# Block-sparse attention with a gated feed-forward: edge rows scored by four 64 by 64 tiles in two halves with a running maximum, and the next batch's keys loaded three units sooner

## Chip, cores and metric

One core of one Trainium2 chip runs the whole program in one launch. The metric is device time in microseconds (us).

## What is computed

Attention with a block mask over 4 batches, 8 heads, 768 positions of width 64 in 24 blocks of 32, and then a gated feed-forward over all 3072 tokens (width 512, inner width 2048):

```python
mask = np.abs(blk_i - blk_j) <= window                      # window = 1
mask = mask | (blk_i == 0) | (blk_j == 0) | (blk_i == n_blocks - 1) | (blk_j == n_blocks - 1)
for qb in range(n_blocks):
    for kb in sampled_blocks[qb]:                           # 3 random blocks of each
        mask[qb * block:(qb + 1) * block, kb * block:(kb + 1) * block] = True
scores = np.where(mask, scale * q @ k.T, -1e9)
attn = softmax(scores)
x = attn @ v                                                # heads side by side: 512 wide
h = x @ w_in
g = h * erf(maximum(h, 0) + log1p(exp(-abs(h))))            # softplus inside erf
out = g @ w_out
```

The 22 middle blocks of queries see eight blocks of keys each. The first and the last block see all 768 keys; these 64 queries of each head are the edge rows.

## The kernel before

**Units.** Each batch is cut into 15 units, in this order: eleven middle units (`"m"`, two middle blocks of queries, all eight heads) and four edge units (`"f"`, one pair of heads each). Below, m0 to m10 are the middle units of a batch and f0 to f3 its edge units; the m0 of the next batch follows f3. A unit goes through these steps: `scores` (L613) has TensorE write f32 scores into the tile `s`, of which there is only one buffer (`ps_s`, `bufs=1`); `soft_max` (L557) has VectorE reduce them to the negated row maxima `less`; `soft_exp` (L566) has ScalarE write `pf = exp(s + less)` and the f16 high part `p`; `soft_low` (L602), one group of the feed-forward later, has VectorE write the f16 low part of `p` and SyncE issue the transposing DMA to `pT`. Three units later `values` (L643) multiplies `pT` with the gathered values into `po`, and `norm` and `turn` make the transposed input `xT` of the feed-forward of it. The two first edge units are answered by `values` together, and so are the two last ones.

**Scores of an edge unit.** Queries and keys lie with two heads on the 128 partitions (64 rows each). For an edge unit a tile `qm`, zero off its diagonal blocks, holds the edge queries of both heads of a pair side by side; `order_q` (L167) fills it once a batch. One matmul of full height and width gives 128 rows (two heads by 64 queries) for 512 keys, a second one those for the last 256 keys (`scores`, the `else` branch). In f32 each of these stands as two instructions in the trace. Middle units use 64 by 32 tiles of the array (eight at a time).

**Groups.** The feed-forward runs in 96 groups (4 batches, 3 chunks, 8 groups). Group m does `ff_first` (24 matmuls into `h`, three buffers), `ff_logs` (five activations of ScalarE: tiles `x` and `y`), `ff_power` (VectorE, `y<-y,x`), `ff_exp` (ScalarE, `y<-y`); two groups later `ff_gate` (VectorE, `y<-y,h`, then two instructions that write `g`), which frees the buffer of `h`; three groups later `ff_second` (12 matmuls into `o`). Of some groups `ff_store` has ScalarE write `wi` or `wo` from `o` and send them out.

**Order of the work.** From the fourth group on (`held[0]`, L983) every engine keeps the order in which the loop from L978 on is written; for the queues of SyncE and GpSimd that holds from the beginning, and before that point a scheduler may move instructions of the other engines. A table (`until`, `spread`, L968 to L975) says which groups carry a unit. A group with a unit runs through

```python
values; ff_first; ff_logs; gathers; scores; ff_second; ff_gate; soft_low(the unit before)
norm; soft_max; turn; ff_power; soft_exp; ff_exp; next_queries; behind
```

so on ScalarE the two activations of `soft_exp` stand between the five of `ff_logs` and the one of `ff_exp`, and on VectorE `soft_low` stands ahead of `soft_max` and `ff_power`.

**The next batch.** `behind` (L853) prepares batch c while batch c - 1 runs. Values: `load_v` (768 KB, ScalarE's DMA queue), `max_v`, `scale_v`, and four `split_v`, at units m10, f0, f2 and f3, each with two activations of ScalarE and two instructions of VectorE into the tile `vn` (one buffer) and a store to a table in memory. Keys: `load_k` (L123) loads four tiles `kr` (384 KB each, one a unit, ScalarE's DMA queue) and `order_k` (L134) has GpSimd copy each into `kx` one unit later. `k_from` (L851) sets the first load at m9; `v_from` sets the first load of values at m6. `kr` has its room in the ring of `pf` (two buffers). When all four are copied, `gathers` may copy random blocks of keys from `kx` into `kbuf`. The `kx` of the second batch lies in the buffer `room`, which holds constants and scratch of the start.

## Time and profile before

| what | us |
|---|---|
| median of 3 runs | 773.09 |
| lowest and highest of them | 768.38, 774.7 |
| the profiled execution: its own time | 770.67 |
| its span, first to last instruction | 768.8 |
| TensorE (PE) busy | 689.5 |
| ScalarE (ACT) busy | 591.9 |
| VectorE (DVE) busy | 575.3 |
| GpSimd (POOL) busy | 202.1 |

The span is that of the profiled execution; 1.87 us of its own time lie outside it. Busy time is the time in which an instruction of the engine ran; TensorE's ends are modelled, since matmuls overlap. PEld is TensorE's loading of weights, and a name with a q (ACTq, SPq) is the sequencer that issues DMAs. Every row carries the line L48, a helper's, so instructions are told apart by the tiles they write and read (`out<-in`). What the names mean: `s_m` and `s_f` are scores of middle and edge units, `po` the attention output, `h` and `o` the two products of the feed-forward.

### The profile page before, as it was taken

What the parts mean: (1) busy time and instruction counts of PE and PEld (TensorE: products, weight loads), DVE (VectorE), ACT (ScalarE), POOL (GpSimd) and SP (SyncE); (2) the same over time, 40 slices, a digit from 0 to 9 for tenths busy, and PEclk for the clock granted to TensorE, in tenths of its full rate; (3) what the DMA queues carried; (4) which work ended last, traced back from release to release, by engine and by line L of the source; (5) the groups of instructions that cost most, each with busy time, mean ns of one, the idle gap of its engine ahead of it and who ended that gap; (6) DMA issues with size and microseconds to landing.
All of it is one profiled execution on the core that took longest, in us unless ns stands there. A gap on an engine that the chain in (4) does not pass through costs nothing.

```text
span 768.8 us, 24885 instructions
## 1 busy us (share of the span) xinstructions
PE 689.5 (90%) x10400; PEld 451.1 (59%) x10400; DVE 575.3 (75%) x1122; ACT 591.9 (77%) x1023; POOL 202.1 (26%) x413
## 2 busy tenths in 40 slices
PE   1347896999899999999899999999999999999997
PEld 0224464656466665666566666666666666667663
DVE  6985999887768878777777878777777786664453
ACT  3546899878868878788878887878878887786774
POOL 3027532214343322031533322033433120000000
PEclk9757997999999999999999999999999999999999
DMA  9999835996799898745988899727979786130000
GB/s 319 411 279 289 248 101 130 195 235 166 145 204 195 209 190 192 189 116 121 227 176 192 169 195 193 210 62 191 214 151 190 137 152 153 42 71 8 8 29 27
DMA packets 188048, 129.36 MB, mean 168 GB/s; under 512 B 137760, under 2 KB 160928, under 8 KB 186912
## 3 DMA queue, kind: packets, MB, share of 16 engines
q1 hardware_dynamic: 173584, 84.50, 52.7%
q10 hardware_dynamic: 8464, 25.43, 10.2%
q0 software_dynamic: 5888, 17.84, 9.1%
q8 instruction: 81, 1.33, 0.7%
q14 instruction: 31, 0.25, 0.1%
HBM read 82.81 MB, written 12.95 MB: 125 GB/s over the span
## 4 chain that ended last, share of the span: by engine, by line
PE 64%; DVE 10%; ACT 8%; DMA 8%; issue 5%; SPq 2%; ACTq 1%; POOL 0%; POOLq 0%; DVEq 0%
PE h L48 26%; PE o L48 25%; PE s_m L48 6%; PE po_None L48 3%; DMA vtab<-vn 3%; DMA vbuf<-vtab 3%; ACT x L48 2%; SPq L48 2%; PE s_f L48 2%; DVE y L48 2%; DVE vn L48 1%; ACT pf_m L48 1%; DMA qt<-in_qT_dram 1%; ACT wi L48 1%; DVE room L48 1%
## 5 line engine op out<-in xcount | busy, mean ns | idle before, releaser
L48 PE MATMUL h<-xT,wi 128*128 128x256 f16 x2304 | 270.7, 274 | 10.5 <-DVE y L48 9.4
L48 PE MATMUL o<-wo,g 128*128 128x512 f16 x1152 | 265.8, 381 | 0.5 <-DVE g L48 0.2
L48 PEld LDWEIGHTS <-wi 128*128 128x128 f16 x2304 | 223.2, 98 | 50.6 <-issue 7.3
L48 ACT ACTIVATE x<-x 128x512 f32<-128x512 f32 x288 | 181.6, 632 | 8.8
L48 PEld LDWEIGHTS <-g 128*128 128x128 f16 x1152 | 109.9, 98 | 129.0 <-issue 10.0
L48 POOL DMA_INDIRECT vbuf<-vtab,idx x88 | 93.8, 1066 | 186.9 <-PE po_None L48 128.1
L48 DVE SCALAR_TENSOR_TENSOR y<-y,x 128x512 f32<-128x512 f32 x96 | 66.9, 697 | 82.0 <-ACT x L48 78.8
L48 POOL COPY kbuf<-kx 128x128 f32 (+1 forms) x280 | 90.3, 367 | 97.1 <-PE s_m L48 82.5
L48 ACT ACTIVATE x<-h,isg 128x512 f32<-128x512 f32 x96 | 65.4, 682 | 50.7 <-PE h L48 32.8
L48 ACT ACTIVATE y<-y 128x512 f32<-128x512 f32 x96 | 59.8, 623 | 36.9 <-DVE y L48 36.9
L48 ACT ACTIVATE pf_m<-s_m,less_m 128x256 f32<-128x256 f32 x176 | 68.9, 473 | 20.9 <-DVE less_m L48 20.9
L48 DVE SCALAR_TENSOR_TENSOR g<-y,sums,g 128x512 f16<-128x512 f32 x96 | 73.0, 761 | 3.4
L48 DVE SCALAR_TENSOR_TENSOR y<-y,h 128x512 f32<-128x512 f32 x96 | 65.1, 678 | 0.1
L48 ACT ACTIVATE y<-x 128x512 f32<-128x512 f32 x96 | 60.5, 631 | 3.0
L48 DVE TENSOR_REDUCE less_m<-s_m 128x4 f32<-128x1024 f32 x44 | 53.5, 1216 | 12.2 <-PE s_m L48 12.2
L48 PE MATMUL s_m<-kbuf,qt 64*32 64x160 f32 x1408 | 51.1, 321 | 4.7 <-issue 3.8
L48 PE MATMUL s_m<-kx,qt 64*32 64x96 f32 x1408 | 31.9, 260 | 23.8 <-ACT kx L48 13.8
L48 PEld LDWEIGHTS <-pT_m 128*32 128x32 f16 x3168 | 35.3, 98 | 28.3 <-issue 25.2
L48 DVE TENSOR_SCALAR g<-y,sums 128x512 f16<-128x512 f32 x96 | 49.2, 512 | 3.4
L48 PE MATMUL po_None<-vbuf,pT_m 128*32 128x65 f16 (+2 forms) x3168 | 41.9, 205 | 7.5 <-issue 7.5
L48 DVE SCALAR_TENSOR_TENSOR p_m<-pf_m,p_m 128x1024 f16<-128x1024 f32 x38 | 46.3, 1218 | 0.6 <-ACT p_m L48 0.6
L48 DVE TENSOR_TENSOR x<-xf,x 128x256 f16<-128x256 f32 x44 | 18.7, 424 | 33.5 <-ACT x L48 33.4
(110 smaller groups left out, 609.9 us busy)
## 6 DMA issues: line engine op xcount, KB each, us to landing
vbuf<-vtab SPq DMA_DIRECT2D x80, 195.0 KB
vraw<-in_v_dram ACTq DMA_DIRECT2D x9, 768.0 KB
vtab<-vn SPq DMA_DIRECT2D x16, 390.0 KB
vbuf<-vtab SPq DMA_DIRECT2D x12, 520.0 KB
wo<-in_w_out_dram ACTq DMA_DIRECT2D x6, 1024.0 KB
qt<-in_qT_dram SPq DMA_DIRECT2D x20, 256.0 KB
kr<-in_kT_dram ACTq DMA_DIRECT2D x12, 384.0 KB
vbuf<-vtab SPq DMA_DIRECT2D x32, 130.0 KB
```

Of the source, the lines that this page charges most:

```text
L48: done = call(*args, **kwargs)
```

## The change

Edge units change in what they hold. A pair of units now covers four heads (two pairs of heads): the even one (f0, f2) scores the first 512 keys, the odd one (f1, f3) the last 256. Each has four matmuls of 64 rows and 64 columns, one for each quarter of the array, read from the queries as loaded; `qm` and `order_q` are gone. The maximum runs: the odd unit takes the smaller `less` of the two, and `drop`, the exponential of the difference (two tiny activations), scales the even unit's `pf`. The f16 high parts of both units are now written in the odd unit's `soft_exp`, both low parts and both transposes come in its `soft_low`, and the even unit has only its exponentials.

```diff
-        dve.tensor_reduce(less, s.rearrange("p (g w) -> p g w", w=width), AX.X, ALU.max, negate=True)
-        dve.tensor_scalar(less, less, D**-0.5, None, ALU.mult)
-        softs[unit] += (less,)
+        dve.tensor_reduce(less, s.rearrange("p (g w) -> p g w", g=groups)[:, :, :width], AX.X, ALU.max, negate=True)
+        if unit[0] == "m" or unit[2] % 2 == 0:
+            dve.tensor_scalar(less, less, D**-0.5, None, ALU.mult)
+            softs[unit] += (less,)
+            return
+        first = softs[unit[0], unit[1], unit[2] - 1][-1]
+        dve.scalar_tensor_tensor(less, less, D**-0.5, first, ALU.mult, ALU.min)
+        dve.tensor_tensor(first, less, first, ALU.subtract)
+        softs[unit] += (less, first)
...
+        if rest:
+            drop = st.tile([P, 2], F32, tag="drop", name=f"drop_{tag}", bufs=1)
+            act.activation(drop, rest[0], AF.Exp)
+            act.activation(drop, drop, AF.Copy, scale=P_SCALE)
...
+            for who, src, scale in ((before, softs[before][0], drop), (unit, pf.rearrange("p (g w) -> p g w", w=width), None)):
...
+                if scale is None:
+                    act.activation(p3[:, :, 0], src, AF.Copy, scale=P_SCALE)
+                else:
+                    for g in range(2):
+                        act.activation(p3[:, g, 0], src[:, g], AF.Copy, scale=scale[:, g : g + 1])
...
+        if unit[0] == "f":
+            if unit[2] % 2 == 0:
+                return
+            for n, (who, p2, p3, src, scale) in enumerate(softs.pop(unit)):
+                if scale is None:
+                    dve.scalar_tensor_tensor(p3[:, :, 1], src, P_SCALE, p3[:, :, 0], ALU.mult, ALU.subtract)
+                else:
+                    for g in range(2):
+                        dve.scalar_tensor_tensor(p3[:, g, 1], src[:, g], scale[:, g : g + 1], p3[:, g, 0], ALU.mult, ALU.subtract)
+                pT = at.tile([P, 16, P], F16, tag="pT", name="pT_" + "_".join(str(x) for x in who), bufs=3)[:, : p2.shape[1] // P]
+                sp.dma_start_transpose(out=pT, in_=p2)
...
-            q_ = qm[:, n].rearrange("p n a c -> p (n a c)")
-            for c, e in ((0, 512), (512, S)):
-                keys = kx[:, c // BLOCK : e // BLOCK, n, :]
-                pe.matmul(s[:, c:e], q_, keys, start=True, stop=True)
-            softs[unit] = (s[:, :S], 1, S)
+            qt = queries(b, NU).rearrange("p r j c -> p r (j c)")
+            first, last = ((0, 16), (16, NB))[n % 2]
+            width = (last - first) * BLOCK
+            for a in range(2):
+                pr, o = n // 2 * 2 + a, slice(a * D, (a + 1) * D)
+                for r in range(2):
+                    d = slice(r * D, (r + 1) * D)
+                    keys = kx[d, first:last, pr, :]
+                    pe.matmul(s[o, r * 512 : r * 512 + width], qt[d, pr], keys, start=True, stop=True)
+            softs[unit] = (s, 2, width)
```

The keys of the next batch start at m6, as its values do, and their tiles `kr` move from the ring of `pf` to the one buffer of `vn`. In `behind` a copy of keys now stands ahead of the steps for values.

```diff
-            kr = at.tile([P, 1024], F32, tag="pf", name=f"kr_{b}_{pr}", bufs=2)[:, :S]
+            kr = at.tile([P, S], F32, tag="vn", name=f"kr_{b}_{pr}", bufs=1)
...
-    k_from = {c: 9 if c == 1 else c * per - 6 for c in range(1, B)}
+    k_from = v_from
```

How the order stands now, at three places. ScalarE in the group that carries f3 of the first batch (`wo` and `out_dram` are the store before it, `x_1_3` and `y_1_3` its group, `vn` the split of values), before and then now:

```order
186 L48 ACTIVATE wo<-o_1_1874,iso_1_2904 128x512
187 L48 DMA out_dram<-wo 128x512
188 L48 ACTIVATE x_1_3_2933<-h_1_3_2908,isg_1390 128x512
...
191 L48 ACTIVATE x_1_3_2933<-x_1_3_2933 128x512
192 L48 ACTIVATE pf_f_3_3007<-s_f_3_2982,less_f_3_3003 128x768
193 L48 ACTIVATE p_f_3_3009<-pf_f_3_3007 128x768
194 L48 ACTIVATE y_1_3_2937<-y_1_3_2937 128x512
195 L48 ACTIVATE vn_0_1_3012<-vraw_0_2687,s_v_2314 128x6x64 x2
```

Now the same group reads:

```order
195 L48 ACTIVATE x_1_3_2981<-h_1_3_2956,isg_1388 128x512
...
198 L48 ACTIVATE x_1_3_2981<-x_1_3_2981 128x512
199 L48 ACTIVATE drop_f_3_3016<-less_f_2_2879 128x2
200 L48 ACTIVATE drop_f_3_3016<-drop_f_3_3016 128x2
201 L48 ACTIVATE pf_f_3_3019<-s_f_3_2988,less_f_3_3011 128x256 x2
202 L48 ACTIVATE p_f_2_3022<-pf_f_2_2887,drop_f_3_3016 128x512 x2
203 L48 ACTIVATE p_f_3_3025<-pf_f_3_3019 128x2x256
204 L48 ACTIVATE y_1_3_2985<-y_1_3_2985 128x512
205 L48 ACTIVATE vn_0_1_3028<-vraw_0_2737,s_v_2321 128x6x64 x2
```

Between the last of the logarithms and `y` stood two activations and stand seven now. VectorE in the next group, from the two instructions that write `g` to the maxima of m0 of the next batch (`po_11_0`, `xf_11` are the norm of f0 and f1), now:

```order
318 L48 SCALAR_TENSOR_TENSOR g_1_2_3210<-y_1_2_2927,sums,g_1_2_3210 128x512
319 L48 SCALAR_TENSOR_TENSOR p_f_2_3022<-pf_f_2_2887,drop_f_3_3016,p_f_2_3022 128x512 x2
320 L48 SCALAR_TENSOR_TENSOR p_f_3_3025<-pf_f_3_3019,p_f_3_3025 128x2x256
321 L48 TENSOR_SCALAR rinv_11_0_3220<-po_11_0_3035 128x2
...
325 L48 TENSOR_REDUCE less_m_0_3226<-s_m_0_3164 128x4
326 L48 TENSOR_SCALAR less_m_0_3226<-less_m_0_3226 128x4
327 L48 SCALAR_TENSOR_TENSOR y_1_4_3161<-y_1_4_3161,x_1_4_3157 128x512
```

Before, one instruction of 768 columns (`p_f_3`) stood where these three of 512 stand. ScalarE at the start of the program, where the scheduler still moves instructions (`raw` and `wo` are loads of weights, `kr_0` the first load of the second batch's keys), now:

```order
23 L48 DMA raw_284<-in_w_out_dram 128x1024
24 L48 ACTIVATE sq_i_501,sums<-wi 128x1024
25 L48 DMA wo<-in_w_out_dram 128x2x1024
26 L48 DMA kr_0_1471<-in_kT_dram 128x768
27 L48 ACTIVATE sq_i_684,sums<-wi 128x1024
28 L48 ACTIVATE pf_m_2_628<-s_m_2_592,less_m_2_625 128x256 x4
```

Row 26 is new there; before, that load stood in the group of m9.

## Rows read from the trace of the kernel before

**Rows 1.** Page, part 1: busy time, share of the span and instructions.
```profile
PE 689.5 (90%) x10400; PEld 451.1 (59%) x10400; DVE 575.3 (75%) x1122; ACT 591.9 (77%) x1023; POOL 202.1 (26%) x413
```
**Rows 2.** Busy time by stretch: us, then each engine; clock, DMA share, GB/s last.
```profile
300.00:345.00 45.00, 43.46 (x483) 28.92 (x481) 33.87 (x69) 36.00 (x60) 8.46 (x21) 1.00 0.66 163
625.00:680.00 55.00, 54.99 (x612) 36.26 (x610) 39.13 (x77) 44.23 (x73) 1.42 (x2) 1.00 0.51 103
55.00:60.00 5.00, 0.69 (x12) 0.28 (x3) 1.74 (x2) 0.00 (x0) 4.08 (x10) 0.50 1.06 263
```
**Rows 3.** Waits of TensorE: who waited for whom, us in total, times, longest.
```profile
PE h L48 <- DVE y L48: 9.4, 4, 4.5
PE s_m L48 <- ACT pf_m L48: 5.4, 3, 2.7
```
**Rows 4.** TensorE in order of time: start, duration, xcount; second batch, m7 and f0.
```profile
261.75 0.56 PE L48 MATMUL s_m<-kx,qt 64*32 64x96 f32 x32
...
309.28 1.46 PE L48 MATMUL s_f<-kx,qm 128*128 128x512 f32 x4
310.57 2.75 PE L48 MATMUL o<-wo,g 128*128 128x512 f16 x12
```
**Rows 5.** Loading of weights around the same two units; idle before in brackets.
```profile
261.75 0.35 PEld L48 LDWEIGHTS s_m<-kx,qt 64*32 64x32 f32 x32 [0.21 <-issue]
...
263.11 0.33 PEld L48 LDWEIGHTS <-g 128*128 128x128 f16 x3 [0.25 <-issue]
...
309.18 0.30 PEld L48 LDWEIGHTS s_f<-kx,qm 128*128 128x128 f32 x2
```
**Rows 6.** Groups by shape: busy us, mean ns of one, idle before.
```profile
L48 ACT ACTIVATE pf_f<-s_f,less_f 128x768 f32<-128x768 f32 x16 | 14.2, 890 | 5.2 <-DVE less_f L48 5.2
L48 ACT ACTIVATE p_f<-pf_f 128x768 f16<-128x768 f32 x16 | 13.5, 843 | 0.5
L48 ACT ACTIVATE x<-x 128x512 f32<-128x512 f32 x288 | 181.6, 632 | 8.8
L48 ACT ACTIVATE x<-xf 128x256 f16<-128x256 f32 x44 | 17.7, 402 | 4.2 <-DVE xf L48 4.1
L48 DVE TENSOR_REDUCE less_m<-s_m 128x4 f32<-128x1024 f32 x44 | 53.5, 1216 | 12.2 <-PE s_m L48 12.2
L48 DVE TENSOR_REDUCE less_f<-s_f 128x1 f32<-128x768 f32 x16 | 15.2, 950 | 0.3 <-PE s_f L48 0.3
L48 DVE SCALAR_TENSOR_TENSOR p_f<-pf_f,p_f 128x768 f16<-128x768 f32 x16 | 15.3, 955 | 0.0
L48 DVE COPY qm<-qt 64x256 f32<-64x256 f32 x8 | 2.3, 285 | 0.1
```
**Rows 7.** In order of time, first border: f3 of batch 0 to the next m1.
```profile
187.03 1.46 PE L48 MATMUL s_f<-kx,qm 128*128 128x512 f32 x4
...
190.28 0.69 ACT L48 ACTIVATE x<-h,isg 128x512 f32<-128x512 f32 x1 [0.43 <-ACT wo L48]
...
195.71 1.10 ACT L48 ACTIVATE vn<-vraw,s_v 128x384 f16<-128x384 f32 x2
...
196.41 1.18 DVE L48 SCALAR_TENSOR_TENSOR vn<-vraw,s_v,vn 128x384 f16<-128x384 f32 x2 [2.07 <-ACT vn L48]
...
199.44 0.95 DVE L48 SCALAR_TENSOR_TENSOR p_f<-pf_f,p_f 128x768 f16<-128x768 f32 x1
...
202.79 1.57 ACT L48 ACTIVATE pf_m<-s_m,less_m 128x256 f32<-128x256 f32 x4 [2.75 <-DVE less_m L48]
...
204.41 0.56 PE L48 MATMUL s_m<-kx,qt 64*32 64x96 f32 x32 [2.71 <-ACT pf_m L48]
```
**Rows 8.** In order of time, second border: the group of m0 and the next m1.
```profile
360.58 0.63 ACT L48 ACTIVATE y<-y 128x512 f32<-128x512 f32 x1 [0.92 <-DVE y L48]
...
368.24 0.56 PE L48 MATMUL s_m<-kx,qt 64*32 64x96 f32 x31 [0.79 <-issue]
```
**Rows 9.** Chain that ended last, at the start of the program: start, us, what.
```profile
52.76 8.99 DMA vbuf<-vtab
```

More of the change, by code (lines that the diff above doesn't have):

```diff
@@ L145, in sparse_attention_moe @@
     qts = {}
-    qm = cp.tile([P, HP, 2, 2, BLOCK], F32, tag="qm", name="qm")
-    dve.memset(qm, 0.0)
     def load_q(b, t):
@@ L165, in queries @@
         return qts[b, t][:, :, half * 2 * BLOCK : (half + 1) * 2 * BLOCK].rearrange("p r (j c) -> p r j c", c=BLOCK)
-    def order_q(b):
-        qt = queries(b, NU)
-        for a in range(2):
-            dve.tensor_copy(qm[a * D : (a + 1) * D, :, :, a, :], qt[a * D : (a + 1) * D])
     QW = 4 * VW
@@ L561, in soft_max @@
         less = st.tile([P, 4], F32, tag="less", name=f"less_{tag}")[:, :groups]
-        dve.tensor_reduce(less, s.rearrange("p (g w) -> p g w", w=width), AX.X, ALU.max, negate=True)
-        dve.tensor_scalar(less, less, D**-0.5, None, ALU.mult)
-        softs[unit] += (less,)
+        dve.tensor_reduce(less, s.rearrange("p (g w) -> p g w", g=groups)[:, :, :width], AX.X, ALU.max, negate=True)
[7 more added lines that the diff above has]
+        softs[unit] += (less, first)
     def soft_exp(unit, early=False):
-        s, groups, width, less = softs[unit]
+        s, groups, width, less, *rest = softs[unit]
         tag = "_".join(str(x) for x in unit)
         n = groups * width
+        if rest:
+            drop = st.tile([P, 2], F32, tag="drop", name=f"drop_{tag}", bufs=1)
+            act.activation(drop, rest[0], AF.Exp)
+            act.activation(drop, drop, AF.Copy, scale=P_SCALE)
         pf = at.tile([P, 1024], F32, tag="pf", name=f"pf_{tag}", bufs=2)[:, :n]
@@ L573, in soft_exp @@
             c = slice(g * width, (g + 1) * width)
-            act.activation(pf[:, c], s[:, c], AF.Exp, bias=less[:, g : g + 1], scale=D**-0.5)
+            act.activation(pf[:, c], s.rearrange("p (g w) -> p g w", g=groups)[:, g, :width], AF.Exp, bias=less[:, g : g + 1], scale=D**-0.5)
         if early:
             softs[unit] = (s, groups, width, pf)
+            return
+        if unit[0] == "f":
+            if not rest:
+                softs[unit] = (pf.rearrange("p (g w) -> p g w", w=width), less)
+                return
+            before = unit[:2] + (unit[2] - 1,)
+            parts = []
+            for who, src, scale in ((before, softs[before][0], drop), (unit, pf.rearrange("p (g w) -> p g w", w=width), None)):
+                w = src.shape[2]
+                p2 = at.tile([P, 2048], F16, tag="p2", name="p2_" + "_".join(str(x) for x in who), bufs=2)[:, : 4 * w]
+                p3 = p2.rearrange("p (g a w) -> p g a w", a=2, w=w)
+                if scale is None:
[3 more added lines that the diff above has]
+                        act.activation(p3[:, g, 0], src[:, g], AF.Copy, scale=scale[:, g : g + 1])
+                parts.append((who, p2, p3, src, scale))
+            del softs[before]
+            softs[unit] = parts
             return
@@ L602, in soft_low @@
     def soft_low(unit):
+        if unit[0] == "f":
+            if unit[2] % 2 == 0:
+                return
+            for n, (who, p2, p3, src, scale) in enumerate(softs.pop(unit)):
[6 more added lines that the diff above has]
+                sp.dma_start_transpose(out=pT, in_=p2)
+                pts[unit[0], unit[1], unit[2] // 2, n] = pT
+            return
         p2, p3, pf3, n = softs.pop(unit)
@@ L665, in values @@
                             else:
-                                pT = pts["f", b, pr][:, x * KT + k]
+                                pT = pts["f", b, p2_, k // 4][:, r * (8 - k // 4 * 4) + x * (4 - k // 4 * 2) + k % 4]
                                 vg = vgs[b, -1 - k // 2][:, k % 2, w]
-                                col = j * 64 + r * BLOCK
+                                col = a * 64 + j * BLOCK
                             todo.append((2 * a + j, pT[:, col : col + BLOCK], vg, at_gr + off))
@@ L836, in next_queries @@
         b, n = divmod(m, per)
-        if n == NU - 1:
-            order_q(b)
         if n < NU - 1 and n % 2 == 0 and (b or n >= 6):
@@ L850, in sparse_attention_moe @@
     v_from = {c: 6 if c == 1 else c * per - 9 for c in range(1, B)}
-    k_from = {c: 9 if c == 1 else c * per - 6 for c in range(1, B)}
+    k_from = v_from
     def behind(m):
         for c in range(1, B):
+            n = m - k_from[c]
+            if 1 <= n < 5:
+                order_k(c, n - 1)
             e = m - v_from[c]
@@ L868, in behind @@
                 have_v.add(c)
-            n = m - k_from[c]
-            if 1 <= n < 5:
-                order_k(c, n - 1)
             if 0 <= n < 4:
```

## Prediction

> **What bounds the kernel now.** I read the busy times first, then the stretches with edge units, then TensorE's waits, and last, in order of time, the borders between batches. TensorE is busy 689.5 of 768.8 us, ScalarE 591.9 [rows 1]. In the edge units of the second batch TensorE works 43.46 of 45 us and ScalarE 36.00; in those of the last batch TensorE works 54.99 of 55 [rows 2]. So TensorE sets the pace, ScalarE is the next engine, and TensorE's waits for others are few: 9.4 us of `h` for a gate of VectorE, 5.4 us of `s_m` for the exponentials that free the one score tile [rows 3]. The question is where these few waits stand: all that TensorE gains ahead of such a wait is lost in it, if what it waits for comes no earlier.
>
> They stand at the borders between batches. At the first one the scores of m1 begin at 204.41, 2.71 us after TensorE was free, when the exponentials of m0 end (202.79 + 1.57 = 204.36) [rows 7]. Those wait for the maxima of VectorE (2.75 us), and VectorE had been held up by `vn`, for which it waited 2.07 us on ScalarE. ScalarE was late already: the scores of f3 begin at 187.03, when TensorE has issued the `h` of that group, but ScalarE takes that `h` at 190.28. At the second border m1 begins at 368.24 after 0.79 us without work [rows 8]; the third repeats it. The last batch has no border behind it.
>
> **TensorE's scores.** An edge unit takes from 309.28 to 310.57, 1.29 us for 768 columns [rows 4], 1.68 ns a column, so 0.86 us for 512 and 0.43 for 256. Do four tiles of 64 by 64 run side by side? The trace shows the neighbouring case: 32 instructions of 96 columns (16 matmuls, eight tiles) take 0.56 us with the tail of the last one [rows 4], while 16 x 96 columns one after the other would take 2.58. So they do, and a pair of units costs 0.86 + 0.43 = 1.29 us where it cost 2.58. With eight pairs that is 10.3 us less. But the weights of the small tiles wait before and after: loading stands idle for 0.21 us ahead of `s_m` and 0.25 behind it, while `s_f` is loaded 0.30 us without a gap [rows 5]. Part of that lies under running matmuls. I take 0.2 us a unit, between nothing and the full 0.46: a pair then saves 1.29 - 0.4 = 0.89, eight pairs 7.1 us (10.3 to 2.9 by the bounds).
>
> The Trainium skill, TensorEngine Tiling (Array Packing), Tiling Modes, says that changing the tiling mode, not just the tile, drains TensorE. The two gaps agree with it, and it speaks against this change: edge units ran in the mode of the feed-forward and would now leave it and come back. Without a drain the sum below would be 0.8 us lower.
>
> **ScalarE.** Before, an edge unit has an exponential of 768 columns (0.89 us) and a copy (0.84) [rows 6], together 1.73. The even unit now has two exponentials of 512, like `x<-x` at 0.63: 1.26, 0.47 less. The odd unit has two of 256 (four take 1.57 [rows 7], so 0.79), three copies of 512 columns (between the 0.40 of 256 and the 0.84 of 768: 0.62 each, 1.86), and two activations of two columns, which no row shows: each costs something between nothing and the 0.40 of 256 columns, and since a fixed part stays I take 0.2. That makes 3.05, 1.3 us more (0.9 to 1.7). A pair costs ScalarE 0.85 us more, in all 6.8 us, off the path as long as ScalarE is not the one waited for.
>
> **VectorE.** Reductions cost 1.216 us for 1024 columns and 0.950 for 768, so 0.68 for 512; the low part costs the same a column (0.955 for 768) [rows 6]. The even unit reduces 0.27 us longer and has no low part (0.955 less). The odd one reduces 0.27 us shorter, adds one tiny instruction, and has three low parts of 512, 2.05 us, 1.1 more. The eight copies into `qm` go (0.285 each); they are followed by `vn`, for which VectorE waits on ScalarE [rows 7], so I count them at nothing, and at most at 2.3 us if that wait is gone.
>
> **What reaches the end, border by border.**
>
> First border. ScalarE's start at 190.28 hangs on a store and the `g` of VectorE, not on TensorE, which is 3 us ahead; what f0 to f2 saved on TensorE does not move it. From there to `vn` at 195.71 ScalarE runs without a pause, so the odd unit moves `vn` by +1.3, and with it VectorE's `vn`, gate and `g`. Then come the low parts at 199.44, 1.1 us longer. The maxima and exponentials of m0, and so m1 at 204.41, come 2.4 us later (0.9 if the small pieces cost nothing and part is caught up, 3.2 at worst).
>
> Second and third border. By the table of units two groups without a unit lie between f1 and f2 and one between f3 and the border, so I take ScalarE to have caught up with TensorE at f2, whose `h` then comes earlier by what f0 and f1 save (0.4 and 0.8, less a little: 1.1). In f3 the odd unit takes 1.3 back, and the longer low parts (1.1) stand ahead of the `y<-y,x` for which ScalarE's `y` waits 0.92 [rows 8]. That is about +0.8 there, of which roughly 0.5 goes into later waits of ScalarE for TensorE's scores: +0.3 each, +0.6 for both (-1.0 to +2.4 each).
>
> Last batch. No border, no split of values, no wait [rows 2]: two pairs at 0.89 give -1.8 (-2.6 to -0.7).
>
> Start. Between loads of weights ScalarE now issues the first keys of the second batch: 128 x 768 x 4 bytes, 393 KB. At that time DMA is full (share 1.06, 263 GB/s [rows 2]) and the chain runs over DMA, the 8.99 us of values for m0 from 52.76 on [rows 9]. 393 KB at 263 GB/s are 1.5 us; some of it goes ahead of that stretch, so I take 1.0 (0 to 3, since the issue itself waits for a store from `vn`, with ScalarE's work queued behind it, and the order of the start is dealt anew).
>
> The Trainium skill, Trainium Kernel Development and Optimization, Key Constraints, says that DMAs from SP, ACT and POOL queues all run on the same 16 engines and interleave. The full share agrees; by it the whole 1.5 us would come out of the start, and the sum would be 0.5 us higher.
>
> Later keys. The loads leave the edge units for m6 to m9, and `kr` has one buffer: a load cannot be issued until GpSimd has copied the tile before, and behind the issue on ScalarE stands the next group. The worst case is the second load, since the first follows 768 KB of values: 1.18 MB at 263 GB/s take 4.5 us, and from f3 to m1, two units, there are 17.4 us [rows 7], so one unit is some 8.7. It fits. I count nothing; if it misses by 2 us three times, ScalarE loses 6 us while TensorE is ahead.
>
> **Sum.** 770.67 + 2.4 + 0.6 - 1.8 + 1.0 = 772.9 us. The profiled execution lies 2.4 us below the median of the runs shown, which spread over 6.3 us, so the forecast is no change: 772.9. A measurement of this kernel can tell about 1% (7.7 us) from no change.
>
> **The rivals.**
>
> *TensorE keeps its saving everywhere.* Then 7.1 us come off: 763.5, and 760.4 without any drain. For it speaks that ScalarE is busy only 36 of 45 us [rows 2] and that `h` waits 9.4 us in the whole run [rows 3]. Against it: the scores of m1 wait for ScalarE at every border already [rows 7, 8], and nothing in the change brings those exponentials forward. It would need ScalarE to catch up 2 us between f3 and m0. Chance 0.17.
>
> *The odd units' tail becomes the bound.* Seven activations and three low parts in one group hold the gate and the next maxima at every border as at the first, and the odd f1 also delays what follows it: 3 x 2.4 + 3 x 1.3 + 1.5 at the start - 1.8 = +10.8, 781.5. It decides from the point at which ScalarE has no pause left between f3 and m0; at the second border 0.92 us of it show [rows 8], at the first none. Against it: after f1 comes a group without a unit in the later batches. Chance 0.18.
>
> *The tiles do not overlap.* If four small matmuls run one behind the other, each as long as a full one, a pair takes 5.16 us and not 2.58: 8 x 2.58 = +20.6, 791.3. Against it stands the row of `s_m` [rows 4]; for it only that no row shows tiles 64 columns wide. Chance 0.03.
>
> **How the numbers follow.** The forecast has the rest, 0.62, and is the only case within 1%. Faster by over 1% is the first rival, 0.17, slower the other two, 0.21. The range goes from 763.5, the saving kept with its drain, to 781.5, the tail at every border; left out are a saving without drain, tiles that do not overlap and a start that costs more than 3 us. The forecast's own range is 768 to 778.
>
> **What the profile after would show.** Right: from the start of `s_f` to the next `o` about 1.06 us in even and 0.63 in odd units; three copies of about 0.62 us in the odd one; at the first border a wait of `s_m` for `pf_m` well over 2.71 us, at the others longer than 0.79; the edge units of the last batch without a wait. Wrong: if m1 begins earlier after f0 than now, counted from m10, then ScalarE had the room and the first rival holds; if `s_f` takes over 1.29 us, the third; if `h` waits for gates several times 9.4 us, the second; if ScalarE stands before m8 or m9 with a load of keys as its releaser, the later keys were not free.

## The result and the profile after

The change takes 777.59 us, median of 13 runs, against 773.09 for the kernel before, also of 13: a ratio of 1.007, 95% interval 1.0046 to 1.0093. One of its 13 executions, at 785.46 us, ran in a slower state; without it the means are 0.6% apart. The change is some 5 us slower than the kernel before: inside the range and inside the 1% that the prediction named, but the interval leaves no doubt of the sign, and the forecast was 772.9 us, no change. Measured again, beside other kernels (e11 below), the ratio was 1.0055 (1.0030 to 1.0080). The profiled execution took 776.47 us, 5.8 more than that of before; its span is 774.7 us, of before 768.8.

The page of after, part 1, answers to [rows 1]:

```profile
PE 680.4 (88%) x10464; PEld 441.2 (57%) x10464; DVE 576.8 (74%) x1129; ACT 597.7 (77%) x1063; POOL 199.6 (26%) x413
```

TensorE has 9.1 us less to do, ScalarE 5.8 us more. All that TensorE was spared is gone, and 5.9 us on top. To find where, the starts of the scores in the two traces are set side by side, unit by unit:

| scores of | before, us | after, us | behind by | gained (-) or lost since the row above |
|---|---|---|---|---|
| f0, first batch | 153.46 | 160.61 | 7.15 | +7.15 |
| f3, first batch | 187.03 | 195.08 | 8.05 | +0.90 |
| m1, second batch | 204.41 | 213.98 | 9.57 | +1.52 |
| f0, second batch | 309.28 | 320.66 | 11.38 | +1.81 |
| f3, second batch | 347.85 | 356.92 | 9.07 | -2.31 |
| m1, third batch | 368.24 | 378.06 | 9.82 | +0.75 |
| f0, third batch | 475.03 | 484.21 | 9.18 | -0.64 |
| f3, third batch | 513.83 | 521.91 | 8.08 | -1.10 |
| m1, fourth batch | 534.25 | 543.05 | 8.80 | +0.72 |
| f0, fourth batch | 639.54 | 647.00 | 7.46 | -1.34 |
| f3, fourth batch | 676.51 | 683.06 | 6.55 | -0.91 |
| end of the span | 768.8 | 774.7 | 5.9 | -0.65 |

The whole loss is there before the first edge unit has begun. What the edge units and borders do afterwards adds up to a small gain. A single row is good to 1 or 2 us only: those from m1 to the next f0 hold no edge unit, and they moved by +1.81, -0.64 and -1.34. In a second trace of the change (e11) the first f0 is 7.64 us behind and the end 5.5. In order of time, TensorE of before and then of after, where the feed-forward begins:

```profile
101.87 3.44 PE L48 MATMUL h<-xT,wi 128*128 128x256 f16 x30 [0.55 <-DVE xT L48]
```

```profile
110.75 5.07 PE L48 MATMUL h<-xT,wi 128*128 128x256 f16 x45
```

The first `h` comes 8.9 us later. The stretch ahead of it, 60 to 90 us (us, then busy time of PE, PEld, DVE, ACT, POOL; clock, DMA share, GB/s), of before and then of after:

```profile
60.00:90.00 30.00, 24.21 (x510) 14.11 (x509) 23.97 (x52) 23.69 (x48) 20.65 (x40) 0.89 1.04 296
```

```profile
60.00:90.00 30.00, 21.70 (x420) 11.68 (x420) 18.49 (x37) 19.05 (x38) 15.99 (x30) 0.76 0.87 245
```

Every engine works 2.4 to 5.5 us less in the same 30 us. What they wait for stands in order of time. Before, 58 to 67 us (`po_None` is the first product with values, `rest` a product of weights, the POOL row the seventh gather of values):

```profile
59.41 2.73 ACTq L48 DMA_DIRECT2D wo<-in_w_out_dram  x2
59.48 0.21 PE L48 MATMUL po_None<-vbuf,pT_m 128*32 128x65 f16 x1 [4.31 <-issue]
...
62.25 1.47 ACT L48 ACTIVATE wi<-wi,sums 128x512 f16<-128x512 f32 x2 [8.91 <-DMA vbuf<-vtab]
63.02 0.58 PE L48 MATMUL rest<-wi,room 128*128 128x512 f16 x1 [2.33 <-ACT wi L48]
...
64.25 1.49 PE L48 MATMUL po_None<-vbuf,pT_m 128*32 128x65 f16 x71
...
66.06 0.97 POOL L48 DMA_INDIRECT vbuf<-vtab,idx  x1 [3.34 <-PE po_None L48]
```

After, 48 to 75 us:

```profile
48.95 0.35 ACTq L48 DMA_DIRECT2D kr<-in_kT_dram  x1
...
58.66 6.47 ACTq L48 DMA_DIRECT2D wo<-in_w_out_dram  x2
...
65.23 1.48 ACT L48 ACTIVATE wi<-wi,sums 128x512 f16<-128x512 f32 x2 [11.59 <-DMA vbuf<-vtab]
66.00 0.58 PE L48 MATMUL rest<-wi,room 128*128 128x512 f16 x1 [10.98 <-ACT wi L48]
...
67.23 0.23 PE L48 MATMUL po_None<-vbuf,pT_m 128*32 128x65 f16 x1
...
67.40 2.50 PE L48 MATMUL rest<-wi,room 128*128 128x512 f32 x3
...
70.55 1.34 PE L48 MATMUL rest<-wi,room 128*128 128x512 f32 x2
...
71.82 0.88 PE L48 MATMUL po_None<-vbuf,pT_m 128*32 128x65 f16 x71
...
73.04 1.81 POOL L48 DMA_INDIRECT vbuf<-vtab,idx  x1 [10.37 <-PE rest L48]
```

Three things are new. The load of keys (`kr`) is out at 48.95, ahead of five of the six loads `wo`. ScalarE's `wi` starts when two of those are issued (62.25 after 59.41 + 2.73 before, 65.23 after 58.66 + 6.47 now), so it seems to stand behind its own sequencer, whatever releaser the row names. And between the first matmul with values and the other 71, which free the buffer for the next gather, TensorE now has five matmuls of weights (67.40 and 70.55) where it had two; that gather starts at 73.04 instead of 66.06. At this point the load and the order are two suspects with one trace; GpSimd's early copy of these keys will be a third.

The edge units themselves. TensorE in the last batch, f2 and f3, answers to [rows 4]:

```profile
676.72 1.09 PE L48 MATMUL s_f<-kx,qt 64*64 64x512 f32 x8
677.74 2.76 PE L48 MATMUL o<-wo,g 128*128 128x512 f16 x12
...
683.06 0.66 PE L48 MATMUL s_f<-kx,qt 64*64 64x256 f32 x8
683.65 2.76 PE L48 MATMUL o<-wo,g 128*128 128x512 f16 x12
```

From the scores to the next `o` 1.02 and 0.59 us, so 1.61 a pair where it was 2.58. Groups by shape of ScalarE, to [rows 6]:

```profile
L48 ACT ACTIVATE p_f<-pf_f,drop_f 128x512 f16<-128x512 f32 x16 | 10.6, 715 | 0.0
L48 ACT ACTIVATE pf_f<-s_f,less_f 128x512 f32<-128x512 f32 x16 | 10.0, 677 | 2.1 <-DVE less_f L48 1.9
L48 ACT ACTIVATE pf_f<-s_f,less_f 128x256 f32<-128x256 f32 x16 | 6.6, 461 | 0.0
L48 ACT ACTIVATE p_f<-pf_f 128x512 f16<-128x512 f32 x8 | 5.0, 621 | 0.0
...
L48 ACT ACTIVATE drop_f<-drop_f 128x2 f32<-128x2 f32 x8 | 1.6, 204 | 0.3
```

And the first border, to [rows 7]: ScalarE's group of f3, VectorE's `vn` and low parts, TensorE's m1.

```profile
197.75 0.69 ACT L48 ACTIVATE x<-h,isg 128x512 f32<-128x512 f32 x1 [0.43 <-ACT wo L48]
...
201.32 0.82 ACT L48 ACTIVATE pf_f<-s_f,less_f 128x256 f32<-128x256 f32 x2
202.03 1.32 ACT L48 ACTIVATE p_f<-pf_f,drop_f 128x512 f16<-128x512 f32 x2
203.25 0.62 ACT L48 ACTIVATE p_f<-pf_f 128x512 f16<-128x512 f32 x1
...
204.29 1.11 ACT L48 ACTIVATE vn<-vraw,s_v 128x384 f16<-128x384 f32 x2
...
204.93 1.23 DVE L48 SCALAR_TENSOR_TENSOR vn<-vraw,s_v,vn 128x384 f16<-128x384 f32 x2 [3.13 <-ACT vn L48]
...
207.99 1.41 DVE L48 SCALAR_TENSOR_TENSOR p_f<-pf_f,drop_f,p_f 128x512 f16<-128x512 f32 x2
...
213.98 0.29 PE L48 MATMUL s_m<-kx,qt 64*32 64x96 f32 x4 [4.38 <-DVE g L48]
```

From ScalarE's first activation to m1 it was 14.13 us and is 16.23; TensorE's wait there grew from 2.71 to 4.38.

### The profile page after: what moved, and what is told of

The parts are those of the page before. It is cut to its first block, busy times and chain, and to the rows that moved or that the text cites. A ratio compares the mean times of both kernels' runs of the same rounds, so it can differ in the third digit from the quotient of the medians.

```text
span 774.7 us, 25067 instructions
## 1 busy us (share of the span) xinstructions
PE 680.4 (88%) x10464; PEld 441.2 (57%) x10464; DVE 576.8 (74%) x1129; ACT 597.7 (77%) x1063; POOL 199.6 (26%) x413
## 2 busy tenths in 40 slices
DMA packets 188050, 129.38 MB, mean 167 GB/s; under 512 B 137760, under 2 KB 160928, under 8 KB 186912
## 3 DMA queue, kind: packets, MB, share of 16 engines
q8 instruction: 82, 1.34, 0.7%
## 4 chain that ended last, share of the span: by engine, by line
PE 54%; DVE 16%; ACT 14%; issue 7%; DMA 5%; SPq 2%; ACTq 1%; POOL 0%; POOLq 0%; DVEq 0%
PE h L48 22%; PE o L48 21%; PE s_m L48 6%; ACT x L48 6%; DVE y L48 3%; PE po_None L48 3%; ACT y L48 3%; DVE g L48 3%; DVE vn L48 2%; SPq L48 2%; DMA vbuf<-vtab 2%; DVE xf L48 2%; DMA vtab<-vn 1%; ACT pf_m L48 1%; DMA qt<-in_qT_dram 1%
## 5 line engine op out<-in xcount | busy, mean ns | idle before, releaser
L48 PE MATMUL h<-xT,wi 128*128 128x256 f16 x2304 | 273.3, 276 | 18.2 <-DVE y L48 15.9
L48 POOL COPY kbuf<-kx 128x128 f32 (+1 forms) x280 | 86.9, 365 | 93.4 <-PE s_m L48 68.3
L48 PE MATMUL s_m<-kbuf,qt 64*32 64x160 f32 x1408 | 48.3, 321 | 3.4 <-issue 2.7
L48 PE MATMUL rest<-wi,room 128*128 128x512 f32 (+1 forms) x48 | 24.2, 618 | 23.5 <-ACT wi L48 12.1
L48 PEld LDWEIGHTS s_m<-kbuf,qt 64*32 64x32 f32 x1408 | 28.7, 111 | 24.0 <-issue 20.6
```

The costliest lines, as they stand in the source:

```text
L48: done = call(*args, **kwargs)
```

## The experiments

All ratios are to the kernel before on the same chip, with the 95% interval; the change itself stands at 1.007 and 1.0055. The medians of e1 to e4, e7, e8 and e13 are of 6 executions, the others of 12.

| run | median, us | ratio | interval |
|---|---|---|---|
| e1 edge scores alone, keys late, tiles in `vn` | 801.93 | 1.0467 | 1.0417 to 1.0516 |
| e2 keys alone | 773.77 | 1.0117 | 1.0066 to 1.0168 |
| e3 second batch's keys late, tiles in `vn` | 782.67 | 1.0183 | 1.0126 to 1.0239 |
| e4 as e3, with an unread load at the start | 786.32 | 1.0269 | 1.0221 to 1.0317 |
| e5 edge scores alone, keys late, own buffer | 772.63 | 0.9996 | 0.9966 to 1.0026 |
| e6 second batch's keys late, own buffer | 773.16 | 1.0015 | 0.9989 to 1.0041 |
| e7 TensorE in written order, with the load | 809.77 | 1.0483 | 1.0446 to 1.0520 |
| e8 TensorE in written order, without it | 808.85 | 1.0477 | 1.0438 to 1.0516 |
| e9 as e6, with the order and no load | 776.64 | 1.0033 | 1.0008 to 1.0058 |
| e10 load as second instruction, own buffer | 780.23 | 1.0079 | 1.0053 to 1.0104 |
| e11 the change again | 778.50 | 1.0055 | 1.0030 to 1.0080 |
| e12 as e6, second batch's keys at m8 | 773.38 | 0.9987 | 0.9960 to 1.0014 |
| e13 as e10, that tile copied late | 775.57 | 1.0106 | 1.0052 to 1.0161 |
| e14 as e10, first copy one unit later | 773.94 | 1.0078 | 1.0049 to 1.0106 |
| e15 as e12, odd unit's copies behind the split | 765.37 | 0.9957 | 0.9924 to 0.9990 |

**The two halves of the change alone (e1 to e4).** e1 is the change with the old starts of the keys. e2 is the kernel before with the keys' part of the change (its second diff, and the copy ahead of the steps for values) and nothing else. The edit of e1:

```diff
-    k_from = v_from
+    k_from = {c: 9 if c == 1 else c * per - 6 for c in range(1, B)}
```

> The change with its edge scores, but the next batch's keys at the old units (m9 to f1 of the first batch, and six units ahead of the border in the others); the key tiles keep their new room in the buffer of vn. Start theory (the early load of keys costs the start 6 to 9 us, the edge scores gain about 3 us in the rest): the start is as before, the first h at about 102 us, and the time is 2 to 4 us under before, 769 to 771. Rival (the odd edge units' tail at the borders costs what was lost): still slower than before, 776 to 778. If the prediction's own sum without its start term holds: +1.2, about 774.

> The kernel before with the keys alone moved (first load at m6, tiles in the buffer of vn, copies ahead of the steps for values); edge scores as before. Start theory: the first h comes at about 111 us and the time is 6 to 9 us over before, 779 to 782, more than the whole change costs, since nothing is won back. Rival (borders): no change, 773.

e3 keeps the later batches early, e4 adds to e3 a load that nothing reads:

```diff
-    k_from = v_from
+    k_from = {c: 9 if c == 1 else v_from[c] for c in range(1, B)}
...
     have_v.add(0)
+    extra = at.tile([P, S], F32, tag="vn", name="extra", bufs=1)
+    act.dma_start(extra, kT[1, 0:2].rearrange("t d s -> (t d) s"))
```

> The whole change, but the keys of the second batch, and only these, start at m9 again; those of the third and fourth batch stay three units sooner. Start theory: first h at about 102 us, the time as with the edges alone, 769 to 771; what differs between the two is what the earlier keys of the later batches give (the prediction counted nothing; up to 2 us either way). Rival (a wait for keys in the later batches): as the change, 777.

> As the run before it, plus one load of the same 393 KB into the buffer of vn at the start, which nothing reads, so that the start of the program has the load but neither the early copy of keys nor its wait for the room of the constants. The order of TensorE at the start is then that of the change, word for word. If the load with the order that it brings is the cost: first h at about 111 us and 776 to 778. If GpSimd's early copy, stuck behind the room of the constants for 15.6 us, is the cost: as without the load, 769 to 771.

e2 bears the start theory out: keys alone cost 9 us (5 to 13 by its interval), with the first `h` at 112.35, and the rival of the borders has no say, since the edge scores are the old ones. e1, e3 and e4 missed all that was expected of them, by more than 30, 10 and 15 us. ScalarE in e3, in order of time at m10 to f1 of the first batch:

```profile
158.23 1.11 ACT L48 ACTIVATE vn<-vraw,s_v 128x384 f16<-128x384 f32 x2
165.68 0.33 ACTq L48 DMA_DIRECT2D kr<-in_kT_dram  x1
166.06 0.69 ACT L48 ACTIVATE x<-h,isg 128x512 f32<-128x512 f32 x1 [6.72 <-DVE less_f L48]
...
178.15 1.12 ACT L48 ACTIVATE vn<-vraw,s_v 128x384 f16<-128x384 f32 x2 [6.73 <-POOL kx L48]
184.31 0.34 ACTq L48 DMA_DIRECT2D kr<-in_kT_dram  x1
184.69 0.69 ACT L48 ACTIVATE x<-h,isg 128x512 f32<-128x512 f32 x1 [5.42 <-DMA vtab<-vn]
```

The tiles of keys and the split values share one buffer, `vn`. With the keys late, a load has to wait until the store of the values has left the buffer, and ScalarE, which issues the load, waits 6.72 and 5.42 us with it; between them a split waits 6.73 us for the copy of keys. The wait for `vtab<-vn` adds up to 22.4 us in e1; the change has none. So the sooner keys were no extra: the new edge scores hold two `pf` from the even to the odd unit, the keys had to leave that ring, and in `vn` they only fit ahead of the splits. Setting one number back was no undoing of one part. Both e3 and e4 have these waits, so e4 can be held against e3: 0.9% more (with 0.75% of uncertainty), though nothing reads the load. But the traces don't show this cost in the start: the third group of `h` begins 3.4 us later in e4 (129.38 against 125.95), the scores of the first f0 do not (156.45 against 156.79).

**The halves with a buffer of their own (e5, e6).** The tiles of keys get 3 KB a partition that nobody shares:

```diff
-            kr = at.tile([P, S], F32, tag="vn", name=f"kr_{b}_{pr}", bufs=1)
+            kr = at.tile([P, S], F32, tag="kr", name=f"kr_{b}_{pr}", bufs=1)
```

> The edge scores alone once more, keys at the old units, but the key tiles get a buffer of their own (3 KB of each partition) instead of the one of vn. In the first try ScalarE stood up to 7.3 us behind a load of keys that waited for a store out of vn. Theory of the shared room: those waits go, f0 to f3 run as in the whole change, and since the start is that of the kernel before, the time is 0.3 to 0.7% under before (ratio 0.993 to 0.997). Rival (the edge scores themselves cost ScalarE and VectorE more than TensorE gains): ratio over 1.005.

> The whole change with a buffer of their own for the key tiles, and the keys of the second batch at m9 as before, those of the third and fourth three units sooner. Start theory: order and transfers of the start are those of the kernel before, so the whole loss goes: ratio 0.990 to 0.997. If sooner keys in the later batches are worth something, it lies under the run with the edge scores alone, by up to 2 us each; the prediction counted nothing for them. Rival (the loss sits at the borders): ratio 1.005 or more, as the change.

Both waits are gone and both kernels take the time of the kernel before. That takes the loss of the change out by changing when the second batch's keys are loaded and copied; the new buffer isn't what does it, since e10 below has it too and loses as the change does. So the loss comes with the early keys of the second batch, and the rival of the borders falls. But e5 and e6 lie above the bands of the start theory, which named a gain besides: the edge scores alone are worth nothing measurable, against an expected gain of 0.3 to 0.7%. e6 against e5 says the same of sooner keys in the later batches: 0.0019, with an uncertainty of 0.004.

**Order or bytes (e7 to e10).** The early load brings two things, 393 KB in a stretch with full DMA, and a start dealt anew. e7 (the change) and e8 (the change with the diffs of e3 and e5) take the dealing away: TensorE keeps the written order.

```diff
-        InOrder(e, queued if e in (nc.sync, nc.gpsimd) else held) for e in (nc.tensor, nc.scalar, nc.vector, nc.gpsimd, nc.sync)
+        InOrder(e, queued if e in (nc.sync, nc.gpsimd) else first if e is nc.tensor else held) for e in (nc.tensor, nc.scalar, nc.vector, nc.gpsimd, nc.sync)
...
+    first[0] = True
     for begun in range(FIRST):
```

> The whole change, but TensorE keeps the written order from the first unit on, so that no scheduler deals its instructions anew at the start; the early load of keys stays. To be read against the next run, which has the same order of TensorE and no early load. If the load's bytes (the gather of values landing 3 us later) are the cost, this run lies 3 to 4 us over the next; if the order dealt anew is (TensorE at its weights ahead of the values, 7 us on GpSimd's gathers), the two lie within 1.5 us of one another. Against before nothing is foretold, since the order itself is another.

> The same written order of TensorE at the start, with the second batch's keys at m9 in a buffer of their own, so no load of keys in the start. If the bytes of the early load are the cost: 3 to 4 us under the run before it; if the order is: within 1.5 us of it.

They lie 0.1% from one another, but with a first `h` at 150 and 147 us this start is some 45 us longer and waits elsewhere. By the time the load is free in that start; in the traces the first f0 is 3.8 us later with it (196.58 against 192.75), and f0 of the second batch only 0.5. On the change's start the pair says nothing. e9 is sharper: one stretch of TensorE's order is held (by `early`, as by `first` in e7) and one step of the weights is moved, in e6.

```diff
     for begun in range(FIRST):
+        if begun == 2:
+            later(1)
...
         gathers()
-        later(3)
+        early[0] = begun == 1
+        later(2 if begun == 2 else 3)
...
                 used_values(place)
+                early[0] = False
```

> As e6 (no load of keys in the start, own buffer for the key tiles, ratio 1.0015 there), but TensorE is held to the written order from the second unit of the start until the first product with values, and one step of the weights is written ahead of that product. So the 72 matmuls of the first product stand behind all six matmuls of weights, as in the change, where five of the six stand ahead of 71 of them; no byte is moved that e6 doesn't move. If the order dealt anew is the cost: GpSimd's seventh gather starts at 71 to 74 us (66 to 71 in the runs with the old order), TensorE reaches the feed-forward some 4 us later, ratio 1.005 to 1.009. If the bytes of the load are: as e6, 0.999 to 1.004.

e10 is the change with the diff of e5, e11 the change unedited. In e10 the load, free of its wait for `vn`, goes out at once.

> The whole change with its early keys for all batches, and a buffer of their own for the key tiles. With nothing to wait for, the first load of the second batch's keys goes out as ScalarE's second instruction of the program, and TensorE's order around the first gather is that of the kernel before. If the order is the cost: ratio 0.997 to 1.003. If 393 KB more in a stretch with full DMA are the cost: 1.5 us by 263 GB/s up to the 3 us by which the gather landed later, so 0.2 to 0.4% over e6, ratio 1.003 to 1.006.

> The change itself, unedited, beside the others on one chip. Both theories: ratio 1.005 to 1.009 as in its first measurement.

e9 comes out between its two values: the seventh gather starts at 69.49, inside the band of the old order, the first `h` at 110.23, as late as in the change, but the third group has made that up again (123.06 in e9, 123.79 in e6, 132.12 in the change). The order alone is worth 0.2 to 0.5% by its two neighbours without it, e6 and e12, and from e6 it can't be told apart. e10 lies above both of its bands: TensorE's old order at the gather, and the full loss of the change. But it doesn't part the order from the bytes, since the scheduler dealt VectorE and ScalarE anew there. VectorE in e10 and then in e12, which take up a load of weights (`room<-wo`) ahead of the first norm (`rinv_None`) and behind it:

```profile
60.71 0.84 DVE L48 TENSOR_SCALAR room<-wo 128x1024 int32<-128x1024 int32 x1 [2.73 <-issue]
...
67.66 0.16 DVE L48 TENSOR_SCALAR rinv_None<-po_None 128x4 f32<-128x4 f32 x1 [3.59 <-PE po_None L48]
```

```profile
68.15 0.16 DVE L48 TENSOR_SCALAR rinv_None<-po_None 128x4 f32<-128x4 f32 x1 [10.97 <-PE po_None L48]
...
68.44 0.66 DVE L48 TENSOR_SCALAR room<-wo 128x1024 int32<-128x1024 int32 x1
```

VectorE's and ScalarE's waits for weights, whole run, in e10:

```profile
ACT sq_o L48 <- DVE wo L48: 7.3, 3, 4.6
DVE room L48 <- DMA wo<-in_w_out_dram: 7.2, 4, 3.3
```

and in e12, which has no load in the start:

```profile
DVE room L48 <- DMA wo<-in_w_out_dram: 3.1, 1, 3.1
...
ACT sq_o L48 <- DVE wo L48: 0.7, 1, 0.7
```

VectorE waits 4 us more for weights and ScalarE 6.6 us more behind VectorE. That the weights land later isn't shown: their last two loads go out at 75.33 and 83.91 us in e10 and at 80.58 and 85.73 in e12, and VectorE comes to `wo` sooner. Nor is it how the change loses its time: there `sq_o` waits 0.8 us for `wo` (0.9 in e11, 1.8 in e2).

**GpSimd's copy, the third suspect (e12 to e14).** In e10 and in the change GpSimd takes up the first copy of keys early and stands 13.5 and 15.6 us for the room of the constants, with the copies and gathers of the next unit behind it. e12 is e6 with an 8 for the 9; e13 is e10 with that copy, and the other three loads and copies of the batch, at their old places; e14 has the copies one unit later:

```diff
+            if c == 1 and n == -3:
+                load_k(c, 0)
-            if 0 <= n < 4:
+            if int(c == 1) <= n < 4:
```

```diff
             n = m - k_from[c]
+            if c == 1 and n > 0:
+                n = n - 1 or -1
             if 1 <= n < 5:
```

> As e6, with the second batch's keys from m8 on instead of m9: the order of the start stays that of the kernel before, and only one of the four loads still falls into an edge unit. In the run with the keys alone the stretch from m10 of the first batch to m1 of the second took 3 us less than before; if sooner keys are worth that, ratio 0.996 to 0.999; by the prediction, which counted nothing, the same as e6, 1.000 to 1.003.

> As e10 (own buffer, first load of the second batch's keys as ScalarE's second instruction), but that tile is copied only at m10, and the other three loads and copies of that batch are at their old units. So the bytes of the early load stay and GpSimd's early copies go. If the bytes are the cost: 1.004 to 1.009, as e10. If GpSimd's copy, which waits 13.45 us for the room of the constants there with six copies and a gather behind it, is the cost: 0.998 to 1.003, as e6 and e12.

> As e10, but the second batch's tiles are copied one unit later (m8 to f0 instead of m7 to m10) and the second to fourth load follow the copies. If GpSimd's wait for the room of the constants is the cost: the copy no longer waits, the copies and gathers behind it start some 7 us sooner, 0.998 to 1.003. If the bytes are: 1.004 to 1.009.

GpSimd's wait is gone in both and the time stays: 1.0106 (over its band, of 6 executions and with a wide interval) and 1.0078. So with the load at the very front the copy is not the cost. These three kernels share the load and an order of VectorE and ScalarE, and in all three `sq_o` waits 6.6 to 7.6 us for `wo`; where the load stands as in the change, the copy is untested by them. e12 shows no gain from keys one unit sooner: 0.9987 lies in the band that named one, but its interval covers both bands.

The start of the first f0's scores, read from every trace but those of e7 and e8, tells more than the times:

| load of the second batch's keys | GpSimd's early copies | traces | first f0, us |
|---|---|---|---|
| none in the start | none | before, e1, e3, e5, e6, e9, e12, e15 | 153.46 to 156.79 |
| behind the first `wo` | yes | the change, e2, e11 | 160.61, 160.64, 161.10 |
| behind the first `wo`, not read | none | e4 | 156.45 |
| ScalarE's second instruction | yes | e10 | 161.40 |
| ScalarE's second instruction | none, or one unit later | e13, e14 | 159.55, 161.21 |

A load at the very front, with the order that comes with it, makes f0 some 5 us late whatever becomes of the copies. In the change's own place one trace has the load without the copies (e4), and there f0 isn't late, so for the change itself the copies are not excluded. e9, with TensorE's order held and no load, isn't late either.

**The tail of the odd unit (e15).** The last term of the sum to be tried: in e12 the two tiny activations and the three copies (the loop over `who`, unchanged) go from ahead of `y` to the end of the group.

```diff
-        if rest:
-            drop = st.tile([P, 2], F32, tag="drop", name=f"drop_{tag}", bufs=1)
-            act.activation(drop, rest[0], AF.Exp)
-            act.activation(drop, drop, AF.Copy, scale=P_SCALE)
...
+    def soft_copy(unit):
+        if unit[0] == "f" and unit[2] % 2:
+            pf, gap, width = softs[unit]
+            drop = st.tile([P, 2], F32, tag="drop", name="drop_" + "_".join(str(x) for x in unit), bufs=1)
+            act.activation(drop, gap, AF.Exp)
+            act.activation(drop, drop, AF.Copy, scale=P_SCALE)
...
             next_queries(begun - 1)
             behind(begun - 1)
+            soft_copy(unit)
```

> As e12 (second batch's keys at m8, own buffer, 0.9987), but an odd edge unit's two tiny activations and three copies on ScalarE (2.35 us) stand at the end of the group, behind y and the split of values, instead of ahead of them. If the odd unit's tail is what TensorE waits for at the first border (m1 waits 4.38 us there in every run with the new edge scores, 2.71 before): VectorE's vn, gate and the next maxima come up to 2.3 us sooner there and about 0.5 to 1 us at the other two, the wait falls to about 2 us, ratio 0.994 to 0.997. If another thing ends last there (the low parts of VectorE, 2.1 us): the wait stays over 4 us and the ratio is 0.997 to 1.001.

0.9957, faster than the kernel before by 0.4%, and than the change by about 1%; beside e12 the 0.3% are no more than the uncertainty, so what the edit itself does is read from the trace. The first border in e15, ScalarE, VectorE and TensorE's m1:

```profile
196.72 0.63 ACT L48 ACTIVATE y<-y 128x512 f32<-128x512 f32 x1
197.26 1.11 ACT L48 ACTIVATE vn<-vraw,s_v 128x384 f16<-128x384 f32 x2
...
197.89 1.15 DVE L48 SCALAR_TENSOR_TENSOR vn<-vraw,s_v,vn 128x384 f16<-128x384 f32 x2 [1.21 <-ACT vn L48]
...
198.73 1.34 ACT L48 ACTIVATE p_f<-pf_f,drop_f 128x512 f16<-128x512 f32 x2
...
206.89 0.56 PE L48 MATMUL s_m<-kx,qt 64*32 64x96 f32 x32 [2.74 <-ACT pf_m L48]
```

The copies now run while VectorE is busy with `vn`, gate and `g`, whose wait for ScalarE fell from 3.13 to 1.21 us. m1 waits 2.74 us and not 4.38, and from f3's scores to m1 it is 17.05 us (before 17.38, after 18.90). At the other two borders the same stretch takes 20.07 and 21.00 us, where it was 20.39 and 20.42 before and 21.14 in the change.

## Why the prediction was wrong

**What bounds the kernel: right.** TensorE works 55.00 of 55 us in the last batch's edge units, and its waits stand at the borders and, as the prediction left out of its list, in the start.

**TensorE's scores: right.** 1.02 and 0.59 us where 1.06 and 0.63 were named, a pair saves 0.97 and not 0.89. The tiles overlap, so the third rival is out. The Trainium skill, TensorEngine Tiling (Array Packing), Tiling Modes, has a change of the tiling mode drain TensorE. The trace fits that, since the saving is 0.32 us short of the 1.29 of tiles without a gap; whether a drain or the loading of the tiles' weights takes them, no run here separates.

**ScalarE and VectorE: right.** Copies 0.66 and 0.62 us (0.62), tiny activations 0.20 (0.2), exponentials 0.82 a pair (0.79); VectorE's low parts 1.41 + 0.69 = 2.10 (2.05).

**First border, +2.4: right.** From ScalarE's first activation in f3 to m1, the stretch that the sum prices, it is 2.1 us (16.23 against 14.13, and 16.22 in e11). In the table of starts f0 to m1 loses 0.90 + 1.52 = 2.4; that this is the very number is luck, since it is 0.8 in e11. e15 takes the copies out of that path, and the wait falls back, so the tail is shown to be the cause.

**Second and third border, +0.3 each: too high.** f3 to m1 loses 0.75 and 0.72, as worked out (+0.8), but f0 to f3 gains 2.31 and 1.10: -1.6 and -0.4, the first of them beyond the -1.0 that was the low bound. It followed a loss of 1.81 at f0, so part of it is only caught up; in e11 the two borders are +0.1 and -0.3.

**Last batch, -1.8: right**, -1.6 by the table and in e11.

**Later keys, nothing: right in size, blind in kind.** No load holds ScalarE up in the later batches of the change, and e6 against e5 shows no difference. But the step took the new place of the tiles for granted; e1 shows that the same place with the old starts costs 37 us.

**Start, +1.0 (0 to 3): the step that failed.** It said that 393 KB at 263 GB/s are 1.5 us, that some of it goes ahead of the full stretch, and so 1.0. Without the early keys of the second batch the kernel takes 0.9996, 1.0015 and 0.9987 of before (e5, e6, e12); with them 1.007 and 1.0055. The difference of the means, 0.0063, is 4.9 us, with about 2 of uncertainty; in the two profiled executions f0 is 7.15 us late. With 4.9 in place of 1.0 the sum is 776.8, 6.1 over the profiled execution of before; that of after is 5.8 over it. That these agree so well is luck: in the traces the start is 7.15, and the second and third border together are -1.9 where the sum has +0.6. The prediction named a full stretch of DMA, an issue that holds ScalarE up and an order dealt anew, but priced the transfer's own time alone; the bound of 3 rests on no row, and a start that costs more was left out of the range without a chance. The trace of after shows the load in the queue ahead of weights (6.47 us from the start of one issue to the end of the next, 2.73 before), ScalarE behind that issue, gathers of GpSimd that wait for weights on TensorE, and a copy of keys for which GpSimd stands 15.6 us; the last two are not in the prediction. The Trainium skill, Trainium Kernel Development and Optimization, Key Constraints, has DMAs from the SP, ACT and POOL queues share the same 16 engines; by it the prediction would have added 0.5 us, and the runs show three times the whole 1.5.

Which of these makes up the 4.9 us stays open. The order that e9 holds, without the load, is worth 0.2 to 0.5% (against e6 and e12), with about 0.4% of uncertainty, and its f0 is not late. The load without that order costs 0.6 to 0.9% (e10 against the same two), but with another order of VectorE and ScalarE. And for the load where the change has it, the copies of GpSimd are not excluded.

**The rivals.** Neither of the first two happened: `h` waits for gates 15.9 us in the whole run, not several times 9.4, and 10.4 of that is one wait in the start; TensorE keeps its saving in the last batch and in part at two borders, and the odd unit's tail is the bound at the first border alone in the size that the second rival gives to all three.

## What to carry to other kernels

A transfer that is moved forward can cost more than its bytes: here 1.5 us of them came with 4.9. Look at where it lands in the queue of its issuer when that issuer also computes, at what still has to come through that queue, and at what else starts sooner with it. Before two runs are read as load against order, set the order of every engine side by side, not TensorE's alone; e10 kept that one around one gather and changed the two others. Before one half of a change is undone, look at which buffers it shares with the other half; here a number set back alone made the kernel 4.7% slower. And work that is needed late should stand at the end of its group, behind what other engines wait for: five activations moved behind the split took 1.6 us off a wait at the border that the new edge scores had made 1.7 us longer.

## What the runs showed of the hardware

A DMA issued by ScalarE can hold its computing up for much longer than the 0.35 to 0.39 us that one issue takes. From the start of one load of weights to the end of the next issue it was 2.73 us before and 6.47 after, and ScalarE's next activation came 0.1 us behind that end both times; a load whose buffer was not free held it for 6.7 us (e3). What the second issue waited for isn't shown. In the list of waits these show as waits for whatever came last (`vbuf<-vtab`, `less_f`), so the sequencer's own row (ACTq) has to be read beside it.

The same 393 KB came with different costs in different starts: 0.6 to 0.9% put ahead of everything (e10 against e6 and e12, where the order of VectorE and ScalarE changed too), and 0.06%, with 0.5% of uncertainty, in a start that is some 45 us longer (e7 against e8).
